# A new order for all 919 steps of an attention and expert-routing kernel

## The chip, the cores and the metric

The kernel runs on one core of a Trainium2 chip. The metric is the device time of one execution in microseconds (us); the median of three runs counts. Engines are named as the profile names them: PE is TensorE (PEld its weight loads), DVE is VectorE, ACT is ScalarE, POOL is GpSimd, SP is SyncE, which issues transfers and computes nothing.

## What is computed

Two stages, all in float32. Attention with sketched features for 4 batches, 4 heads, 1088 tokens and 32 values per head, then a layer of 8 experts in which each of the 4352 tokens goes to one expert:

```python
def phi(x):
    a = np.einsum('rd,bhsd->bhsr', S1, x)          # r = 8
    b = np.einsum('rd,bhsd->bhsr', S2, x)
    return np.einsum('bhsi,bhsj->bhsij', a, b).reshape(*x.shape[:-1], r * r)
q_p, k_p = (phi(q), phi(k))
kv = np.einsum('bhsf,bhsd->bhfd', k_p, v)
z = np.sum(k_p, axis=2)
x = num / den            # num = q_p kv, den = q_p z + 1e-6, as rows of 128
...
logits = x @ w_gate                                 # 128 -> 8
expert_idx = np.argmax(logits, axis=1)
out = gate_w * (np.maximum(x_e @ w1[e], 0.0) @ w2[e])   # 128 -> 1024 -> 128
```

S1 and S2 are float64 and are taken apart into float32 pieces on the chip.

## The kernel before

The kernel is a list of named steps. Each step is a small function that issues a few instructions on fixed engines, and the string `ORDER` at the top of the file names all steps in the order in which they are issued. No scheduler reorders anything: each engine runs its own instructions in the order of that string, and waits where data or a buffer isn't ready. Buffers come from rings (8 PSUM banks, 12 wide buffers of 128 x 1024, 5 buffers for turned rows, and so on), handed out in the order of the string too, so another order also changes which step must be over before a buffer can be used again.

The steps by name:

- `L.…` on SP: a load from HBM. `L.q0`, `L.k1`, `L.v2` are q, k or v of one batch, 512 KB each; `L.kr0a` and the like are the last 64 tokens of a batch, 32 KB; `L.w0` to `L.w7` and `L.x0` to `L.x7` are w1 and w2 of one expert, 512 KB each; `L.fill` writes filler rows into the scratch table. The loads of k of batch 0 (`k0`) stand before the string.
- `S.t`, `S.m`: S1 and S2 are put on the diagonal blocks of a weight (`s_cat`), by two PE transposes (L398) of what a row of DVE instructions made (`s_rep`, L293), and two DVE products (L405).
- `k<batch><half>` and `q<batch><half>` (and `kr`, `qr` for the last tokens): `.t` four PE transposes of the loaded rows (L420), `.x` copy from PSUM (L429 on DVE and L430 on ACT for the first two, ACT alone later), `.a` the products with S1 and S2 on PE (L438), `.l` copy on ACT, `.s` sum on DVE (L453), `.o` outer product on DVE (L466); for k then `.v` on PE (L475, L479), and after a batch's last key the steps `e<batch>`. For q: `.T`/`.U` transposes on PE (L577), `.c`/`.d` copies on ACT, `.n`/`.N` numerators on PE (L595), `.p`, `.e`, `.y` division on ACT and DVE, and `.f`, `.f2` copies of two token columns each into the rows to be routed, on ACT (L622).
- `r<batch>`: routing. `.a` to `.d` give each token its row in a scratch table in HBM that is sorted by expert: `.a`, `.b` on DVE, `.p` on PE (L692, L694), `.d` on DVE (ends with L707), and `.c` (L684 to L686) the gate weight, which stands in the routed row. Then `.s0` to `.s8` scatter the rows, 128 at a time, with indirect transfers on POOL (L713).
- `t<group>` on DVE: which expert and which rows each tile has.
- `j<tile>`: 38 tiles of 128 rows of one expert. Tiles 0 to 9 need the rows of batches 0 and 1, tiles 10 to 17 those of batch 2 as well, later ones all. `.n` reads a row number on SP, `.l` loads and turns the rows (L902), `.g` loads two words of each row (L904), `.c` copies on ACT (L972), `.w` and `.X` copy the expert's w1 and w2 on DVE (L984, L990), `.u` and `.U` are the halves of the first product on PE (L1005), `.r` and `.q` the ReLU on ACT (L1031, L1038) or DVE (L1040), `.d` the second product on PE (L1054), `.y` the scaling on ACT (L1071), `.s` the scatter of the result on POOL (L1076). Tiles 27 to 37 are of two halves of 64 rows each (L1011, L1059).
- `warm` is one PE matmul on zeros after the six of the head; `D0` to `D3` drain POOL; `N2` numbers rows on POOL; `m0.i`, `m1.i` are tiles that run only if they are needed.

The body of a step is short. Two that the prediction speaks of, and the loop that issues them all:

```python
        @op(x + ".l")
        def _():
            if split:
                s["xr"] = xr_bufs.take(2)
                load_rows(j, s["row"], (s["xr"][0:64], slice(0, XW), False))
            else:
                s["t"] = turned_bufs.take()
                load_rows(j, s["row"], (s["t"][:], slice(0, DM), True))
...
    for name in ORDER.split():
        do(name)
```

Of the kernel before, what the change touches and what calls it, by code (L numbers as in the profile page):

```python
# [23 lines left out]
L.k1 k00.o q00.t kr0.a q00.x L.gate q01.x k01.s k11.t L.v0 k01.o kr0.l kr0.s q00.a L.vr0a C.late q00.l L.k3
q01.a L.qr0b q00.s D0 L.v1 k00.v k11.x k01.v kr0.o L.qr0a e0.s q01.l e0.r L.fill e0.k k10.t q00.o k10.x
L.vr1a L.w1 e1.s k11.a q00.U q01.s q01.o q00.T k11.l e0.t C.later e0.c L.qr1a e0.m q01.T q00.c k11.s e0.z
L.q3 q00.d q01.U k10.a q00.N L.q1 q01.c k10.l q01.d q01.n qr0.t L.k2 q00.n q01.p L.q2 q01.N k11.o k10.s
k10.o q00.p2 q01.e q00.e2 L.vr0b qr0.x q00.p q01.y q10.t q11.t qr0.a k20.t q01.p2 q00.y2 q10.x q00.e qr0.l q10.a
q01.e2 q00.y q01.y2 r0.a L.v2 r0.x k10.v k11.v qr0.s q11.x L.kr1b q10.l r0.b q00.f2 k20.x r0.c r0.p L.kr1a
r0.d q10.s e1.r q11.a L.w3 e1.k q11.l k20.a q01.f L.w6 e1.t q00.f q10.o q11.s q10.T qr0.o k20.l q11.o  # L30
q01.f2 q10.U r0.s3 q20.t e1.c e1.m k20.s qr0.T q11.U q20.x qr0.c q11.T L.w0 L.w2 e1.z k20.o q10.c kr1.t
L.v3 qr0.n q10.n L.x2 q11.d qr0.p q11.c L.qr1b q11.N q11.n q10.p q10.d q10.N k21.t qr0.e L.x4 q10.e q11.p2
q10.y q11.e2 q20.a q11.p qr0.y q10.p2 q11.e q11.y2 q20.l q10.e2 r0.s5 L.vr1b r0.s6 r0.s1 kr1.x k21.x r0.s7 q30.t
q11.y q10.y2 r1.a q31.t q11.f2 r1.x kr1.a q21.t k30.t q20.s q11.f kr1.l k21.a L.x1 r1.b q20.o kr1.s k30.x
L.w5 r1.c r0.s4 q10.f2 qr1.t r1.p k30.a r1.d k21.l L.x3 q21.x k20.v k21.s q20.T k30.l qr0.f q20.c kr1.o
e2.s r0.s2 q21.a q30.x k21.o q10.f k21.v q30.a r0.s0 q31.x L.w4 qr1.x k30.s r1.s7 r1.s2 e2.r t0.a k31.t
r1.s1 q20.U q21.l k30.o t0.b e2.k e2.t k31.x k30.v q21.s e2.c k31.a L.w7 q31.a q30.l t0.c q30.s r1.s0
k31.l q21.o e2.m q20.d L.x0 k31.s e3.s e2.z q31.l q30.o q21.U q21.T L.x5 q21.c q31.s q20.n k31.o j8.n
q31.o q20.N q30.T qr1.a q20.p j5.n q21.n qr1.l k31.v q21.p qr1.s e3.r q21.d j5.w q31.U L.x6 e3.k r1.s6
q31.T j7.n q20.e r1.s8 j7.w q30.c e3.t q20.p2 q20.y q21.N r1.s4 j3.n q31.d j9.w e3.m q21.e j0.n q20.e2  # L40
q30.U r1.s3 q21.p2 e3.z q21.e2 j6.n e3.c r1.s5 q30.d j4.n q31.N L.x7 j9.n q30.N qr1.o q21.y q30.p2 q31.c
q30.n q20.y2 j9.l j7.l qr1.T q21.y2 q31.n r2.a j0.l r2.b qr1.c q31.p2 q30.e2 j9.X j9.c qr1.n q31.e2 r2.x
q20.f2 j9.g q30.p r2.p q30.y2 j1.w j3.w j7.c j9.u j9.U D1 j8.w N2 j9.r r2.d j7.u j5.l j0.c
q31.y2 j3.l q20.f j2.n qr1.p j0.X j2.l j0.w qr1.e j4.w q21.f j9.q q30.e j4.X j7.X j7.U j6.l j9.d
q30.f2 j5.c j0.U j3.c r2.c j5.u j7.q j5.g t0.d j5.U j9.y q21.f2 j9.s r2.s6 j7.r t1.a q31.p j1.n
j5.q j5.X j8.l j4.l j1.l j7.g t1.b j5.r t1.c qr1.y q31.e r2.s1 j2.c j0.u j0.q j13.n j3.X j6.w
j6.c q30.y r2.s5 r2.s0 j7.d r2.s7 j0.r j3.U q31.f2 j0.g j6.X j4.c j3.g q31.y j8.c j5.d j2.w j15.n
r3.a j3.u j0.d j6.U j3.q r2.s4 j14.n j1.c j8.u j12.n j0.y j3.r j1.g j1.U q30.f j17.X j10.w j8.U
j6.u j16.n r3.x r2.s3 r3.b j5.y r3.c r3.p j6.g j6.r j16.w j17.w r2.s2 r3.d t1.d j4.u r3.s3 t2.a
j7.y t2.b j10.n j3.d t2.c r3.s1 j4.U qr1.f j2.u q31.f j2.g j8.X j17.n j13.l j6.q j4.r j4.g j2.r  # L50
j17.l j2.U j2.X j17.c j14.w t2.d j10.l j15.w j2.q j4.q j6.d j8.g j17.U j15.l j6.y j2.d j17.u r3.s4
r3.s5 j8.r j18.w r3.s2 j14.l j14.c j17.r j4.d j17.g j20.n r3.s0 j14.u j1.u j22.n j1.X j24.n j17.q j0.s
t3.a j1.q j18.n j11.n t3.b j3.y j14.U j16.l j16.g j17.d j16.c j1.r j16.X r3.s6 r3.s7 j12.l j15.X j10.c
j15.c j26.w j25.n j8.q j26.n r3.s8 j14.r j11.w j18.l j1.d t3.c j17.y j14.X j33.n j33.l j18.c j26.l j1.y
j20.l j15.u j10.u j6.s j15.U j8.d j15.r j26.c j27.n j16.u j16.U j13.X j20.w j14.q j23.n j12.w j18.X j16.q
j22.l j11.l j14.d D2 j16.r j16.d j15.g j29.n j10.g j8.y j31.n j20.c j4.y j20.u j12.X j16.y j20.r j10.U
j10.r j29.l j2.y j19.n t3.d j4.s j15.q j20.X j15.d j20.U j13.w j11.c j31.W j36.n j19.l j18.U j24.g j20.q
j14.g j13.c j31.w j23.l j14.y j26.u j19.c j15.y j11.U j20.g j18.q j20.d j13.U j18.u j31.l j13.g j10.q j22.c
j11.u j26.U j10.X j18.r j32.n j28.n j15.s j11.X j23.c j33.L j11.r j18.d j5.s j29.L j8.s j31.L j33.W j13.q
j27.l j13.u j20.y j34.n j10.d j31.j j1.s m1.w j22.w j12.c j10.y j23.w j12.u j11.q j22.U j2.s j18.g j11.g  # L60
j30.n j21.n j31.o j18.y j26.X j11.d j26.r j29.j j3.s j17.s j29.o j29.X j23.U j27.L j11.y j22.g j32.l j36.l
j12.r j22.u j33.o j37.n j26.q j19.g j13.r j33.j j12.U j13.d j22.q j23.u j26.g j29.W j32.L j34.l j33.b j22.r
j31.b j24.w j24.X j29.b j35.n j21.l j22.X j12.q j31.c j26.d j22.d j21.c j25.X j12.g j33.w j23.q j34.L j19.w
j13.y j12.d j19.X j27.o j36.L j11.s j31.u j31.U j33.c j23.r j20.s j32.o j21.w j33.u j29.w j29.c j31.r j12.y
j22.y j24.l j34.o j33.U j29.U j31.q j26.y j27.w m0.w j29.u j27.j j19.u j32.X j19.U j26.s j32.j j35.l j29.q
j23.X j23.g j24.c j31.X j36.o j16.s j33.X j19.r j31.d j21.u j7.s j33.q j23.d j33.r j24.u j36.j j25.w j35.L
j32.w j30.w j29.r j19.q j28.l j28.L j30.l j24.U j19.d j34.j j25.l j37.l j21.U j21.X j22.s j24.r j28.j j25.c
j35.j j33.d j23.y j24.q j21.r j14.s j25.U j27.W j25.g j37.L j33.y j27.X j31.y j30.L j12.s j25.u j24.d j30.X
# [1104 lines left out]
```

## Time and profile before

| | |
|---|---|
| median of 3 runs | 199.47 us (199.17 to 199.88) |
| the profiled execution's own time | 197.44 us |
| its span, first to last instruction | 195.7 us |
| PE busy | 187.8 us |
| DVE busy | 137.8 us |
| ACT busy | 101.5 us |
| POOL busy | 84.5 us |
| moved by DMA | 23.02 MB |
| granted TensorE clock, mean | 1.00 |

The profiled execution took 1.7 us more than its span and 2.0 us less than the median of the runs. In what follows a time such as "at 62.45" counts from the first instruction of the span. A timeline row gives start, duration, engine, line, operation and names, and in brackets how long the engine stood idle before it and what ended that. Rows that overlap (one engine works on several instructions at a time) are usual: a PE matmul row lasts until its modelled end, while the next one starts well before that.

### The profile page before, as it was taken

To read this page: it belongs to the slowest core of one execution; us is meant where nothing else is said; L and a number is where in the kernel's file an instruction comes from. 1 tells how busy PE (TensorE), PEld (TensorE's weight loads), DVE (VectorE), ACT (ScalarE), POOL (GpSimd) and SP (SyncE) were. 2 spreads that over 40 slices of the span, in tenths; PEclk is the share of its full clock that TensorE was granted. 3 is DMA by queue.
4 is the path that set the end of the run, shared out by engine and by line. 5 is a ranking of instruction groups with operands and counts; after the bars stand their busy time and mean duration, and the time that the engine had idled before them with its cause. 6 is when DMAs were issued, how large, how long until landed. Compare 5 with 4: busy or idle time off the path is not lost.

```text
span 195.7 us, 8926 instructions
## 1 busy us (share of the span) xinstructions
PE 187.8 (96%) x3609; PEld 180.7 (92%) x3609; DVE 137.8 (70%) x406; ACT 101.5 (52%) x255; POOL 84.5 (43%) x106
## 2 busy tenths in 40 slices
PE   7999999998999999999999999999999999999991
...
DMA packets 35660, 23.02 MB, mean 118 GB/s; under 512 B 17155, under 2 KB 33413, under 8 KB 35617
## 3 DMA queue, kind: packets, MB, share of 16 engines
...
q8 instruction: 30, 0.49, 1.1%
...
HBM read 15.84 MB, written 5.05 MB: 107 GB/s over the span
## 4 chain that ended last, share of the span: by engine, by line
PE 69%; DMA 11%; issue 5%; POOL 5%; DVE 3%; ACT 1%; POOLq 1%; SPq 1%; DVEq 0%; ACTq 0%
PE bank L1054 22%; PE bank L1005 21%; PE bank L1011 8%; PE bank L1059 7%; DMA turned<-xs_dram 5%; POOL xs_dram L713 4%; PE bank L438 4%; DMA wide<-in_k_dram 3%; PE bank L420 2%; DMA xs_dram<-x_rows,row_i 2%; PE bank L577 2%; PE bank L475 1%; POOL out_dram L1076 1%; PE bank L595 1%; SPq L902 1%
## 5 line engine op out<-in xcount | busy, mean ns | idle before, releaser
L1076 POOL DMA_INDIRECT out_dram<-y,xg x27 | 29.6, 1096 | 61.2 <-ACT y L1071 55.4
L1005 PE MATMUL bank<-xgT,wide 128*64 128x128 f32 x864 | 51.6, 273 | 0.4 <-ACT xgT L972 0.3
L713 POOL DMA_INDIRECT xs_dram<-x_rows,row_i x34 | 38.6, 1135 | 24.8 <-DVE sum L453 10.4
L1005 PEld LDWEIGHTS bank<-xgT,wide 128*64 128x64 f32 x864 | 47.8, 137 | 0.9 <-ACT xgT L972 0.9
L1040 DVE TENSOR_SCALAR hTb<-bank 128x512 f32<-128x512 f32 x26 | 17.8, 687 | 31.4 <-PE bank L1011 8.5
L984 DVE COPY wide<-w_all 128x1024 f32 x45 | 30.8, 704 | 8.2 <-PE bank L1054 4.4
L1031 ACT ACTIVATE hTa<-bank 128x512 f32<-128x512 f32 x36 | 21.2, 596 | 27.0 <-PE bank L1011 10.4
L1054 PE MATMUL bank<-wide,hTa 128*64 128x128 f32 x432 | 28.3, 273 | 0.2 <-ACT hTa L1031 0.2
L1054 PE MATMUL bank<-wide,hTb 128*64 128x128 f32 x432 | 28.2, 273 | 0.0
L1054 PEld LDWEIGHTS bank<-wide,hTa 128*64 128x64 f32 x432 | 24.3, 137 | 0.7 <-ACT hTa L1031 0.4
L1054 PEld LDWEIGHTS bank<-wide,hTb 128*64 128x64 f32 x432 | 24.5, 137 | 0.0
L990 DVE COPY wide<-w_all 128x1024 f32 x27 | 18.4, 698 | 2.9 <-PE bank L1054 2.2
L466 DVE TENSOR_TENSOR wide<-sum 128x1024 f32<-128x1024 f32 (+1 forms) x18 | 20.2, 1129 | 0.3
L972 ACT COPY xgT<-turned 128x256 uint16<-128x256 uint16 x27 | 12.6, 482 | 13.9 <-DMA turned<-xs_dram 13.8
L438 PE MATMUL bank<-s_cat,xT 128*128 128x128 f32 x136 | 18.5, 280 | 0.2 <-DVE se L684 0.2
L1011 PE MATMUL bank<-xgT,wide 128*64 128x64 f32 x576 | 17.5, 222 | 0.0
L1011 PEld LDWEIGHTS bank<-xgT,wide 128*64 128x64 f32 x576 | 17.3, 138 | 0.2 <-issue 0.2
L438 PEld LDWEIGHTS bank<-s_cat,xT 128*128 128x128 f32 x136 | 16.4, 191 | 0.6 <-ACT x_rows L622 0.2
L1071 ACT ACTIVATE y<-bank,xg 128x128 f32<-128x128 f32 x27 | 9.6, 368 | 11.7 <-PE bank L1054 8.0
L1076 POOL DMA_INDIRECT out_dram<-y,to x11 | 10.8, 978 | 7.7 <-ACT y L1071 5.0
L430 ACT COPY xT<-bank 128x512 f32<-128x512 f32 (+2 forms) x20 | 9.7, 503 | 4.3 <-PE bank L420 4.0
L595 PE MATMUL bank<-kvx,q_pT 128*64 128x82 f32 x272 | 11.5, 237 | 0.1
...
## 6 DMA issues: line engine op xcount, KB each, us to landing
...
xs_dram<-x_rows,row_i POOLq DMA_INDIRECT x34
turned<-xs_dram SPq DMA_TRANSPOSE x27
xg<-xs_dram SPq DMA_DIRECT2D x27, 1.0 KB
```

What stands on the lines that cost most here:

```text
L438: nc.tensor.matmul(t[:, ts(i, 128)], lhsT=st["xT"][:, ts(i, 128)], rhs=s_cat.rearrange("p w t g r -> p (w t g r)"), start=True, stop=True)
L466: nc.vector.tensor_tensor(dst, a[:, :, :, None].broadcast_to([128, n * 4, R, R]), b[:, :, None, :].broadcast_to([128, n * 4, R, R]), ALU.mult)
L713: d = nc.gpsimd.indirect_dma_start(out=xs_dram[:], out_offset=bass.IndirectOffsetOnAxis(ap=st["row"][:, u:u + 1], axis=0), in_=x_rows[b][: ...
L984: nc.vector.tensor_copy(out=s["w1", i], in_=w1_all[:, ds(expert(i), F)])
L990: nc.vector.tensor_copy(out=s["w2"], in_=w2_all[:, ds(expert(0), F)])
L1005: nc.tensor.matmul(t[ts(g, 64), ts(c, 128)], lhsT=s["w1", 0][:, ds((c0 + c) * 128 + g * 64, 64)], rhs=s["xT"], start=True, stop=True, skip ...
L1011: nc.tensor.matmul(t[ts(g, 64), ds(c * 128 + i * 64, 64)], lhsT=s["w1", i][:, ds((c0 + c) * 128 + g * 64, 64)], rhs=s["xT"][:, ts(i, 64)], ...
L1031: nc.scalar.activation(s["hTa"], s["ha"], AF.Relu)
L1040: nc.vector.tensor_scalar(s["hTb"], s["hb"], 0.0, None, ALU.max)
L1054: nc.tensor.matmul(t[ts(i, 64), :DM], lhsT=h[:, ds(c % 4 * 128 + i * 64, 64)], rhs=s["w2"][:, ts(c, DM)], start=(c == 0), stop=(c == 7), s ...
L1059: nc.tensor.matmul(t[ts(i, 64), :DM], lhsT=h[:, ds(c % 4 * 128 + i * 64, 64)], rhs=s["w2"][:, ts(c, DM)] if i else w2_all[:, ds(r + c * DM ...
L1076: d = nc.gpsimd.indirect_dma_start(out=out[:], out_offset=bass.IndirectOffsetOnAxis(ap=s["xg"][:, 1:2].bitcast(I32), axis=0), in_=s["y"], ...
```

## The change

Only the string `ORDER` changes. The same 919 names stand in it, in another order, so that every engine has the same instructions as before in another row. The first line of the string, before and after:

```diff
-warm k00.t k00.x S.t S.m k01.t L.q0 L.kr0a k00.a k01.x L.kr0b k00.l k01.a q01.t k00.s kr0.t k01.l kr0.x
...
+warm S.t k00.t k01.t L.q0 L.kr0b L.kr0a k00.x S.m k01.x L.k1 k00.a L.qr0b k01.a q00.t k00.l L.gate k00.s
```

Three places of it, as the built programs have them.

PE at the head of the program; `wide_73` is k of batch 0, `s_rep` what S1 and S2 became. Before:

```order
L255 MATMUL bank_65<-zeros 128x128 x6
L255 MATMUL bank_66<-zeros 128x128
L420 MATMUL bank_67<-ident,wide_73 128x128 x2
L420 MATMUL bank_68<-ident,wide_73 128x128 x2
L398 MATMUL bank_69<-ident,s_rep_261 128x16
L398 MATMUL bank_69<-ident,s_rep_264 128x16
L420 MATMUL bank_70<-ident,wide_73 128x128 x2
L420 MATMUL bank_71<-ident,wide_73 128x128 x2
L438 MATMUL bank_72<-s_cat,xT_85 128x128 x4
```

and now:

```order
L255 MATMUL bank_65<-zeros 128x128 x6
L255 MATMUL bank_66<-zeros 128x128
L398 MATMUL bank_67<-ident,s_rep_261 128x16
L398 MATMUL bank_67<-ident,s_rep_264 128x16
L420 MATMUL bank_68<-ident,wide_73 128x128 x2
L420 MATMUL bank_69<-ident,wide_73 128x128 x2
L420 MATMUL bank_70<-ident,wide_73 128x128 x2
L420 MATMUL bank_71<-ident,wide_73 128x128 x2
L438 MATMUL bank_72<-s_cat,xT_85 128x128 x4
```

The first four transposes of k (`k00.t`) have moved behind the two of S (`S.t`).

SP's queue of loads from the load of v of batch 0 on (in each line the loaded tensor stands at the right). Before:

```order
L186 DMA wide4_77<-in_v_dram 128x4x256
L191 DMA v_rem_170<-in_v_dram 64x4x32
L186 DMA wide6_79<-in_k_dram 128x4x256
L191 DMA q_rem_169<-in_q_dram 64x4x32
L186 DMA wide7_80<-in_v_dram 128x4x256
L191 DMA q_rem_169<-in_q_dram 64x4x32
L375 DMA xs_dram_166<-x_rows3_182 9x8x1040
L191 DMA v_rem_170<-in_v_dram 64x4x32
L364 DMA w1_all_172<-in_moe_w1_dram 128x1024
L191 DMA q_rem_169<-in_q_dram 64x4x32
L186 DMA wide10_83<-in_q_dram 128x4x256
L186 DMA wide11_84<-in_q_dram 128x4x256
```

and now:

```order
L186 DMA wide4_77<-in_v_dram 128x4x256
L191 DMA v_rem_170<-in_v_dram 64x4x32
L191 DMA q_rem_169<-in_q_dram 64x4x32
L375 DMA xs_dram_166<-x_rows3_182 9x8x1040
L186 DMA wide6_79<-in_q_dram 128x4x256
L364 DMA w1_all_172<-in_moe_w1_dram 128x1024
L191 DMA k_rem_168<-in_k_dram 64x4x32
L186 DMA wide7_80<-in_q_dram 128x4x256
L186 DMA wide8_81<-in_k_dram 128x4x256
L186 DMA wide9_82<-in_q_dram 128x4x256
L186 DMA wide11_84<-in_v_dram 128x4x256
```

Before, k of batch 3, v of batch 1, w1 of expert 1 and q of batch 3 stand ahead of q of batch 1 (`wide11_84`, the last row). Now q of batch 3 (`wide6_79`) and w1 of expert 0 alone stand between v of batch 0 and q of batch 1 (`wide7_80`); k and q of batch 2 follow, then v of batch 1.

POOL from the numbering of batch 2's rows (L239) on; `row_i_2` and `row_i_3` are the scatters of batches 2 and 3, `out_0_dram` those of results. Before:

```order
L239 IOTA x_rows0_223 128x8
L1076 DMA out_0_dram<-y0_154,xg0_107 4352x128
L713 DMA xs_dram_166<-x_rows0_223,row_i_2_1331 39168x130 x8
L713 DMA xs_dram_166<-x_rows3_182,row_i_3_1702 39168x130 x6
L1076 DMA out_0_dram<-y1_155,xg3_110 4352x128
L713 DMA xs_dram_166<-x_rows3_182,row_i_3_1702 39168x130 x3
```

and now:

```order
L239 IOTA x_rows0_223 128x8
L713 DMA xs_dram_166<-x_rows0_223,row_i_2_1327 39168x130 x8
L713 DMA xs_dram_166<-x_rows3_182,row_i_3_1708 39168x130 x4
L1076 DMA out_0_dram<-y0_154,xg2_109 4352x128
L1076 DMA out_0_dram<-y3_157,xg0_107 4352x128
L713 DMA xs_dram_166<-x_rows3_182,row_i_3_1708 39168x130 x5
```

The result of the first tile (`j9.s`) no longer stands ahead of the eight scatters of batch 2.

In the same stretch the other engines read as follows in the string, cut to the steps that matter. PE after the first tile's first product: before `j7.u j7.U j9.d j0.U j5.u j5.U j0.u j7.d j3.U j5.d j3.u j0.d j6.U j8.u j1.U j8.U j6.u r3.p j4.u j3.d j4.U j2.u j2.U j6.d j17.U`, now `j7.U j7.u j9.d j3.U j0.U j3.u j0.u j7.d j8.u j3.d j8.U j6.U j4.U j0.d j4.u r3.p j2.U j6.u j8.d j17.U`. ACT: before `j9.c r2.x q20.f2 q30.p j7.c j9.r j0.c q20.f qr1.p q21.f j9.q q30.f2 j5.c j3.c j7.q j9.y q21.f2`, now `q20.f q31.d q31.p r2.x qr1.c q21.f2 q30.p2 j9.c j7.c qr1.p j9.r j9.q q30.p q21.f q20.f2 j0.c`. DVE: `r2.c` stood 18 steps behind `r2.a`, and now stands 8 behind it. SP's loads of turned rows: before `j9.l j7.l j0.l … j13.l j4.g j17.l`, now `j9.l j7.l j3.l … j14.l j17.l`.

## Rows read from the trace of the kernel before

**Rows 1.** The page: busy tenths of PE in 40 equal slices of the span.

```profile
PE   7999999998999999999999999999999999999991
```

**Rows 2.** Waits of PE's weight loads: who for whom, us in total, times, longest.

```profile
PEld bank L1005 <- ACT xgT L972: 0.9, 2, 0.5
PEld bank L475 <- issue: 0.8, 1, 0.8
...
PEld bank L420 <- DMA wide<-in_q_dram: 0.4, 1, 0.4
PEld bank L1054 <- ACT hTa L1031: 0.4, 1, 0.4
PEld bank L420 <- DMA wide<-in_k_dram: 0.4, 1, 0.4
```

**Rows 3.** Chain that ended last, in order of time: start us, us, what.

```profile
53.19 3.28 DMA xs_dram<-x_rows,row_i
...
57.94 3.96 DMA turned<-xs_dram
61.92 0.49 ACT xgT L972
...
62.45 1.97 PE bank L1005 x32
```

**Rows 4.** Timeline of PE at the head: start, us, engine, line, operation.

```profile
4.21 0.69 PE L420 MATMUL bank<-ident,wide 128*128 128x128 f32 x4
...
5.73 0.66 PE L420 MATMUL bank<-ident,wide 128*128 128x128 f32 x4
6.25 0.49 PE L438 MATMUL bank<-s_cat,xT 128*128 128x128 f32 x2
```

**Rows 5.** Timeline of DVE at the head, and its row at 20.99.

```profile
5.44 0.40 DVE L429 COPY xT<-bank 128x256 f32<-128x256 f32 x1
5.84 0.35 DVE L405 TENSOR_TENSOR s_cat<-bank,mask 128x64 f32<-128x64 f32 x2
...
20.99 0.89 DVE L615 TENSOR_TENSOR heads_of<-bank,den_q 128x320 f32<-128x320 f32 x2 [0.45 <-PE bank L595]
```

**Rows 6.** Timelines: batch 0's last scatter, batch 1's first, DVE's step before it.

```profile
38.09 1.25 POOL L713 DMA_INDIRECT xs_dram<-x_rows,row_i  x1 [0.30 <-issue]
40.69 1.87 POOL L713 DMA_INDIRECT xs_dram<-x_rows,row_i  x1 [1.34 <-issue]
...
39.69 0.23 DVE L707 TENSOR_REDUCE row_i<-rk 128x9 int32<-128x72 f32 x1
```

**Rows 7.** Timeline of POOL: batch 2's first and last scatter.

```profile
68.80 0.98 POOL L713 DMA_INDIRECT xs_dram<-x_rows,row_i  x1 [0.68 <-DVE done L819]
...
78.64 1.01 POOL L713 DMA_INDIRECT xs_dram<-x_rows,row_i  x1 [0.30 <-issue]
```

**Rows 8.** Timelines of DVE (the end of `r2.c`) and ACT (a copy `.f2`).

```profile
67.71 0.21 DVE L686 RECIPROCAL x_rows<-se 128x8 f32<-128x8 f32 x1 [0.23 <-DVE se L685]
...
64.66 0.63 ACT L622 COPY x_rows<-heads_of 128x512 uint16<-128x512 uint16 x1
```

**Rows 9.** Timelines of SP and ACT: tiles 13 and 17 turned, tile 17's copy.

```profile
82.47 1.20 SPq L902 DMA_TRANSPOSE turned<-xs_dram  x1
...
84.50 2.53 SPq L902 DMA_TRANSPOSE turned<-xs_dram  x2
...
87.07 0.49 ACT L972 COPY xgT<-turned 128x256 uint16<-128x256 uint16 x1 [0.48 <-DMA turned<-xs_dram]
```

**Rows 10.** Chain that ended last: one second product, then half a first product.

```profile
69.66 1.75 PE bank L1054 x32
71.40 0.87 PE bank L1005 x16
```

**Rows 11.** Scatters into the table (ns: least, median, most); DVE at 3.05.

```profile
L713 POOL DMA_INDIRECT xs_dram<-x_rows,row_i x34: 966/988/1907, 27.4 to 94.9; - x34
...
3.05 1.44 DVE L272 TENSOR_SCALAR expo_at<-expo 16x32 int32<-16x32 int32 x1
```

More of the change, by code (lines that the diff above doesn't have):

```diff
@@ L22 @@
 ORDER = """
-warm k00.t k00.x S.t S.m k01.t L.q0 L.kr0a k00.a k01.x L.kr0b k00.l k01.a q01.t k00.s kr0.t k01.l kr0.x
[L24 to L68, printed above, removed]
@@ new lines @@
+k01.l kr0.t k00.o L.v0 q01.t k01.s kr0.x L.vr0a kr0.a q00.x kr0.l k01.o q00.a kr0.s q01.x L.qr0a k11.t e0.s
+q00.l q01.a L.fill L.q3 L.w0 k00.v L.kr1b k11.x L.q1 L.k2 k01.v C.late L.q2 D0 kr0.o q00.s e0.r q00.o
+q01.l e0.k qr0.t k11.a L.v1 q01.s e0.t L.vr0b e0.c q01.o k10.t C.later q01.T k11.l k10.x L.k3 L.qr1a L.kr1a
+q01.c q00.U q00.d L.w2 q01.U k10.a k11.s qr0.x e1.s e0.m q01.d L.vr1b e0.z L.w6 L.x1 k11.o q00.T k10.l
+k10.s q01.n q01.N q00.c q01.p k10.o q00.N q01.p2 q00.n q00.p2 q00.p q01.e q01.e2 q10.t qr0.a L.x5 k20.t q11.t
@@ new lines @@
+q10.x qr0.l q01.y q01.y2 q00.e2 q00.e L.qr1b q01.f q00.y2 q00.y L.v2 q20.t q11.x r0.a r0.x q10.a qr0.s k20.x
+r0.b r0.c k10.v r0.p q11.a r0.d r0.s4 q01.f2 L.x3 k11.v q10.l e1.r L.w7 q10.s k21.t q11.l q00.f e1.k
+k20.a e1.t r0.s0 q10.o qr0.o q11.s q20.x k20.l q11.o e1.c r0.s6 qr0.T e1.m q00.f2 q10.T q11.U k20.s q11.T
+q10.U qr0.c q10.c L.x4 e1.z q11.d qr0.n qr0.p q11.N q10.n q11.c q11.p2 q10.d k20.o q11.n q10.p q11.p q10.N
+L.v3 r0.s1 qr0.e qr0.y q11.e2 q11.y2 L.w1 qr1.t q10.e kr1.t q10.y q20.a k21.x q10.p2 L.w3 q11.e q20.l q11.y
@@ new lines @@
+q10.e2 q30.t k30.t q21.t L.vr1a qr0.f q10.y2 r1.a kr1.x q20.s k30.x r1.b q10.f k21.a r1.x k31.t q20.o r1.p
+k31.x q11.f r0.s2 L.w4 L.x7 kr1.a r1.d r0.s7 k21.l q10.f2 k31.a r0.s3 r1.c q20.T r0.s5 k21.s t0.a q31.t
+k20.v q20.c r1.s5 L.w5 q30.x kr1.l q21.x kr1.s k30.a e2.s q21.a k21.o k30.l k21.v q11.f2 k30.s q30.a L.x6
+e3.s L.x2 q21.l q31.x t0.b r1.s1 kr1.o q21.s qr1.x t0.c e2.r q20.U j6.n q30.l k30.o q30.s e2.k r1.s3
+e2.t q21.o k31.l j8.n q31.a k30.v k31.s e2.c q21.T e2.m q21.U q20.d e2.z q30.o r1.s7 q20.N k31.o q31.l
@@ new lines @@
+q21.d qr1.a q31.s j9.w j3.n q20.n q21.N q30.U q21.c k31.v q21.p2 j3.w j4.n j9.n qr1.l j5.n j2.n r1.s0
+e3.r r1.s6 q30.T r1.s2 q21.e2 j1.n L.x0 q31.o e3.k q20.p2 r1.s8 j0.n q20.e2 q20.p qr1.s e3.t qr1.o q30.d
+q21.n q21.y2 e3.m q31.T q20.e j7.n q21.p e3.z q20.y2 q31.U e3.c q20.y q30.N q21.e q30.c q21.y q31.c r1.s4
+r2.a j9.l q20.f q31.n qr1.T q30.n q31.d q31.p q31.e D1 r2.b q31.N r2.x j7.l r2.p q31.y j3.l qr1.c
+q21.f2 q30.p2 j0.l j9.c qr1.n j7.w j9.X j7.c j9.u j9.U qr1.p j6.l j9.r j0.g j9.q r2.d q30.p j7.U
@@ new lines @@
+j7.u j9.d j3.g q21.f q30.e2 r2.c qr1.e j0.w N2 q20.f2 j8.l q30.y2 t0.d j0.c t1.a j7.X j4.l j7.q
+j3.c j8.w t1.b q30.e j3.U j0.U j3.q t1.c j3.u r2.s2 j7.r j2.l q30.y r2.s1 j8.c j17.n r2.s5 q31.p2
+j0.q qr1.y r2.s4 j3.X r2.s6 j3.r j5.l j12.n q31.e2 j4.c j0.X j0.u q30.f2 j9.g qr1.f j15.n j5.g j13.n
+j7.g j6.g r2.s0 j7.d j8.u j1.g q31.y2 j6.w j15.w j3.d j2.w j8.r j14.n j8.U j6.c j2.X j4.w r2.s3
+j5.c j6.U j8.X j0.r j6.q j1.l j2.c j4.U j5.w j0.d r3.a q31.f2 j9.y j1.c j4.q r2.s7 r3.b j14.l
+j17.l j11.w j11.X j17.w j4.u j8.q q30.f j16.n j6.X r3.p j2.U r3.x j7.y j17.c j6.u t1.d r3.d j8.d
@@ new lines @@
+j13.w j17.U j4.X j12.l j6.r t2.a j13.l j15.l j17.g q31.f j6.d j17.q r3.c j1.w r3.s4 j17.X j4.g j13.c
+j2.u j4.r t2.b j17.u j10.n j2.q j15.c j4.d r3.s2 t2.d j8.g r3.s5 j6.y j1.U j17.r t2.c t3.a j15.u
+j12.g r3.s3 j17.d j12.c j0.y j2.r t3.b t3.c j9.s j11.n j0.s j16.l j5.u r3.s8 r3.s7 j5.X r3.s1 j10.l
+j26.w j11.l j16.c j3.y j13.u j5.U j18.n j18.w j17.y r3.s0 j16.w j2.g j13.U j11.c j13.r r3.s6 j4.y j14.g
+j24.n j5.r j33.n j11.U j1.q j20.n j21.n j6.s j5.q j1.u j19.n j23.n j13.X j18.l j15.U j2.d j5.d j15.r
@@ new lines @@
+j25.n j10.c j19.l j23.l j31.n D2 j26.n j1.X j10.w j16.X j11.g j18.g j28.n j31.l j2.y j29.W j1.r j14.w
+j15.q j29.n j11.u j18.c j12.w j16.U j16.u j1.d j13.q j29.w j14.X j8.y j13.g j22.n m0.w j15.g j16.r j16.q
+j13.d j5.y j18.X j23.w j11.r j29.l j11.q j10.U j23.c j16.d j10.u j15.X j12.u j14.c j26.l j30.n j15.d j18.U
+t3.d j1.y j11.d j10.q j12.r j11.y j31.L j10.X j10.g j13.y j10.r j14.U j20.l j12.U j14.u j26.c j22.l j33.l
+j36.n j18.u j33.L j26.U j20.w j22.w j14.q j10.d j32.n j27.n j24.l j15.y j22.c j31.j j26.q j26.u j26.X j8.s
```

19 lines of the change are left out of this document (14 added, 5 removed).

## The prediction, made before the changed kernel ran

> **What bounds the kernel now.** I read the page's slices first. PE is at nine tenths or more in all but three of the 40 slices [rows 1], so the time is its start, its work, the little that it waits and a tail, and an order that changes no instruction can win only waits. Next the waits of its weight loads, which stand at the head of each group of matmuls and so show when PE lacked something. The five largest waits behind the head are 0.9, 0.8, 0.4, 0.4 and 0.4 us, 2.9 us together [rows 2]: about 1.5% of the time, and the most that this change can gain outside head and tail.
>
> Then the chain that ended last, to see who sets those waits. In the attention half it runs through POOL: the scatters of batches 0 and 1, one train of 17, then their landing, the turned load of an expert tile, ACT's copy and PE at 62.45, the second tile's first product [rows 3]. From there PE works almost without a gap to the end, so a microsecond at 62.45 is a microsecond at the end, unless a later wait eats it. The last thing to read is when the next group of tiles, 10 to 17, can be loaded, since these need batch 2's scatters. The tail (last product, scaling, five scatters, landing) holds the same steps in both orders; I take 0 for it.
>
> The sum is made against the profiled execution, 197.44 us. The median of the runs is 199.47, 2.03 more, and I add that at the end. A measurement of this kernel can tell 0.3%, 0.6 us, from no change.
>
> **Head: PE starts 0.72 us later.** Now PE does four transposes of k at 4.21, while DVE still prepares S, and the other four from 5.73, and its first real product starts at 6.25 [rows 4]. With S first, the first four move to 5.73 and the others behind them. By the length of those rows (0.66 us for four) I estimate that the first pair is out at about 6.11. DVE's copy of that half (0.40) and the products that make `s_cat` (0.35) come in this order [rows 5], so `s_cat` is ready at about 6.91, and the product starts at 6.97 instead of 6.25.
>
> **Loads: 0.8 us of waits go.** PE waited 0.4 us for q of batch 1 and 0.4 us for k of batch 2 [rows 2]. Counting 512 KB loads from the start, q of batch 1 was the ninth and is the seventh, k of batch 2 was the tenth and is the eighth. Both waits should close, even with nothing else gained. q of batch 2 is now the ninth and v of batch 1 the tenth, where the ninth and tenth now land just when PE stands at `q10.t` and `k20.t`; PE comes to `q20.t` four and to `k10.v`, the first use of v of batch 1, six steps after `q10.t`, so neither is late. Head and loads together: -0.1 us at the point where the waits were. If the head's loss stayed in full, DVE's steps would carry it on to the scatters below.
>
> **Batch 1's scatters: 0.3 us earlier.** Batch 0's last scatter ended at 39.34 and batch 1's first began at 40.69, after 1.34 us of idling; ordinary idling is 0.30 [rows 6]. It waited for DVE, whose last step ended at 39.92, 0.77 us before. DVE comes there 0.72 later by the head, 0.45 earlier by the wait at 20.99 [rows 5] that goes with the loads, and some 0.2 earlier since one small sum now stands behind it; at best 0.7 more of small gaps close. So the scatters start between 40.04 and 40.76: 0.65 earlier to 0.07 later. I take 0.35 earlier, near the middle, and put PE's 62.45 at 62.1. The instruction fetch that held PE for 0.8 us at line 475 [rows 2] lies beside this train and is taken at zero either way; without that cover it costs or saves up to 0.8.
>
> **Batch 2's scatters: 3.7 us earlier, and needed 5 us earlier.** Before, the train of eight started at 68.80, behind the first tile's result on POOL and behind `r2.c`, which ended at 67.92 [rows 7, 8]. Now nothing of tile 9 stands ahead of it, and `r2.c` is ten steps earlier on DVE, some 4 us. The last thing the first scatter waits for is `q20.f2` on ACT. ACT starts tile 7's copy at 61.92 now [rows 3] and is through the copy, two ReLUs, two row copies and two short ones by 64.66 [rows 8]; the new order has the same kinds in that stretch with one copy fewer. Less the 0.35, that is 64.3. With 0.77 to the first scatter [rows 6] it begins at 65.1.
>
> Today's train has its last start 9.84 us after its first, 1.41 each; at its shortest a scatter takes 0.98 and 0.30 of idling, 1.28 [rows 7]. So the last starts at 74.1 to 74.9. The first turned load of the group followed 3.83 us after the last start (78.64 to 82.47), a second load follows after 1.35, and tile 17's copy started 2.57 after its load [rows 9]; PE starts 0.53 after such a copy (61.92 to 62.45) [rows 3]. That makes tile 17's `.U` possible at 82.4 to 83.2.
>
> PE now comes to it sooner. Between the second tile's start and `j17.U` it did 26 us of work; in the new order 13 halves of 0.87, 5 second products of 1.75 [rows 10] and the routing product, some 0.6: 20.7 us. From 62.1 that is 82.8. So data and PE meet within half a microsecond; I take 82.9. The old kernel had the same amount of work behind it at 62.45 + 20.7 = 83.15. **So the change is 0.25 us ahead there.**
>
> **After that 0.8 us more.** The second of the two waits for turned rows (0.9 in total less the 0.5 at 62.45) and the wait for a ReLU that was stuck behind such a copy, 0.4 each [rows 2], belonged to tiles 14 and 16, whose loads came 3 us after tile 17's and were needed at once. In the new order tiles 15, 13, 11 and 16 follow at 7 to 20 us behind `j17.U`, with loads 1.35 apart; by the same steps each has 1.4 us or more to spare. Batch 3's rows are needed some 30 us later, and `r3.c` may slip by 3 us unseen. DVE's copies of weights are in time by their order in the worst case I found (`j4.w`, about a microsecond ahead). All other moves I take at zero, with their ends at the largest single wait of today, 0.9, either way: every step has a new neighbour, and a new wait of that size needs no special reason.
>
> **The sum:** -0.25 - 0.8 = -1.05; 197.44 - 1.05 = 196.4 in the profile, and with 2.03 **198.4 us**. By the ends of the terms this case alone spans 197.8 to 199.1.
>
> **Rivals.**
>
> *Batch 2's scatters come too late: slower.* The new order has 5.3 us less work to cover their train. If the train is no earlier than now, tile 17 is ready at 82.47 + 1.35 + 2.57 + 0.53 = 86.9, 3.75 us late; less the 0.8 that is 202.4. If it starts on time but each takes as long as in batch 1's train, (53.19 - 40.69) / 8 = 1.56 [rows 3, 6], `j17.U` comes at 84.2: 199.7. The point from which it decides is 1.52 us a scatter. For it: the train now runs beside weight copies on DVE, scatters took up to 1.91 us, and at 3.05, while POOL filled buffers, a DVE step on 16x32 values lasted 1.44 us [rows 11], so the two engines can hold each other up. Against it: today's train also ran beside a busy DVE, at 1.41. I put it at 201.
>
> [...]
>
> *No change.* Batch 1's train starts no earlier (its upper end), tile 17 is half a microsecond late, and the fetch or one of the new neighbours takes back the rest: 199.4. That the order doesn't do what it was searched for belongs here: where the fetches fall among the loads can't be read from it.
>
> *More.* Every term at its good end, the wait of 0.5 at 62.45 gone as well: -0.65 - 0.8 - 0.5, 197.5.
>
> **Chances.** The forecast 0.45, too late 0.20, no change 0.27, more 0.08. Of the forecast's 0.45, 0.38 lies below 198.87 and counts as faster, with "more" and a little of "no change" 0.48. Within 0.3%: 0.07 of the forecast, 0.22 of "no change", 0.02 of the late train, 0.31. Slower 0.21. The range 197.2 to 201.0 leaves out the worst half of the late train and the last of "more".
>
> **What would show it.** The first L438 at about 6.97. No wait of L420 for q or k. Batch 1's first scatter near 40.3. Batch 2's first scatter near 65.1 and its last near 74.5. PE's `j17.U` near 82.9, with no wait of L1005 for a copy above 0.5 and none of L1054 for a ReLU. Wrong would be a train of batch 2 that begins later than 66 or needs over 11 us, or a new wait of a microsecond in the middle of the tiles.

## The result and the profile after

The changed kernel is slower: median 201.66 us over 20 runs (199.81 to 203.11) against 199.38 us over 20 runs of the kernel before on the same chip, a ratio of 1.0121 with an interval of 1.0094 to 1.0148. Forecast was 198.4 us, with a range of 197.2 to 201.0.

| | before | after |
|---|---|---|
| median | 199.38 us | 201.66 us |
| profiled execution, own time | 197.44 us | 201.70 us |
| its span | 195.7 us | 199.9 us |
| PE busy | 187.8 us | 190.1 us |
| POOL busy | 84.5 us | 83.0 us |
| first L438, start | 6.25 | 7.55 |
| batch 1's first and last scatter, start | 40.69, 53.19 | 43.24, 55.25 |
| second tile's first product | 62.45 | 64.55 |
| batch 2's first and last scatter, start | 68.80, 78.64 | 67.38, 77.27 |
| last scatter of a result, start | 192.00 | 196.21 |

The two profiled executions differ by 4.3 us, the medians by 2.3: the profile of before lies 1.9 under its median, that of after on it. So the profiles tell where time went, and the ratios how much. Two of the five sets of runs below met chips whose granted clock was 0.86 to 0.93 in every execution, those of the kernel before too (267 to 275 us): of these runs only the head is read, and their ratios (0.976 to 0.984 for five runs of a_tail, a_all and a_best, 1.011 and 1.019 for b_warm2 and b_warm2b) are not used.

The slices of the changed kernel's page, to be laid beside [rows 1]:

```profile
PE   6999999999999999999899999999999999999990
...
DVE  5399998899998899888899585557484365160210
...
POOL 8010018768820475007771103861001017787453
```

PE is as full as before. POOL is busy at seven to eight tenths from 170 to 185, which will matter for the tail.

**The head.** Timeline of PE in the changed kernel, against [rows 4]:

```profile
1.06 3.35 PE L255 MATMUL bank<-zeros 128*128 128x128 f32 x14 [1.06 <-DVE zeros L201]
5.25 0.61 PE L398 MATMUL bank<-ident,s_rep 16*128 16x16 f32 x2 [0.83 <-DVE rest L298]
5.79 1.97 PE L420 MATMUL bank<-ident,wide 128*128 128x128 f32 x8
7.55 2.88 PE L438 MATMUL bank<-s_cat,xT 128*128 128x128 f32 x16
10.27 0.60 PE L420 MATMUL bank<-ident,wide 128*128 128x128 f32 x4
```

The order of the rows is the forecast's, their lengths are not. Eight transposes take 1.97 us, where four took 0.66; their starts lie 0.213 us apart, the next group's (at 10.27) 0.109. The trace's first record of the granted clock, at full speed, stands at 9.49; in the kernel before at 4.38. In both the pace changes there: the starts of L438 lie 0.213 apart up to 9.47 and 0.111 to 0.112 from 9.60 on, and in the kernel before the transposes from 4.41 on lie 0.109 to 0.110 apart, behind warm-up matmuls at 0.213. So PE did this work at about half the pace of the kernel before. What PE did ahead of it: the warm-up ends at 4.4, and it stood idle for 0.83 us until S came. Before, it went from the warm-up into k's transposes without a pause.

**Batch 1's scatters.** Timeline of DVE in the changed kernel where batch 1's routing ends, against [rows 6]:

```profile
41.65 0.23 DVE L707 TENSOR_REDUCE row_i<-rk 128x9 int32<-128x72 f32 x1
...
42.25 0.22 DVE L686 RECIPROCAL x_rows<-se 128x9 f32<-128x9 f32 x1
```

and of POOL, batch 0's last scatter and batch 1's first:

```profile
40.00 1.98 POOL L713 DMA_INDIRECT xs_dram<-x_rows,row_i  x1 [0.30 <-issue]
43.24 0.97 POOL L713 DMA_INDIRECT xs_dram<-x_rows,row_i  x1 [1.26 <-ACT q_pT L583]
```

The gate weights (`r1.c`, ending with L686) now stand behind the row numbers (`r1.d`, ending with L707), and the scatter needs both. It starts 0.77 after the end of L686 at 42.47, as it started 0.77 after L707 in the kernel before. The bracket names ACT's copy L583, which ended at 43.12. In a_best4 below that copy ended at 42.50, when the first scatter had long started (40.27, again 0.77 after DVE's last step), so the scatter doesn't wait for it.

**The middle.** Waits of PE's weight loads in the changed kernel (who for whom, us in total, times, longest), against [rows 2]:

```profile
PEld bank L1005 <- ACT hTa L1031: 1.4, 1, 1.4
...
PEld bank L1005 <- ACT xgT L972: 0.6, 1, 0.6
```

The chain that ended last, from 78 to 101 us (start us, us, what):

```profile
78.67 2.38 DMA turned<-xs_dram
...
81.68 3.54 DMA turned<-xs_dram
85.22 0.02 issue
85.24 0.48 ACT xgT L972
85.72 0.04 issue
85.77 1.09 PE bank L1005 x16
...
94.83 4.42 DMA turned<-xs_dram
99.25 0.02 issue
99.27 0.02 ACT xgT L972
99.29 0.32 issue
99.62 0.59 ACT hTa L1031
100.21 0.04 issue
100.25 0.76 PE bank L1005 x9
```

No wait for q or k is left, as forecast. The wait of 0.6 is tile 17 at 85.77. The wait of 1.4 is new: tile 11's turned rows, asked for at 94.83, came 4.42 us later; ACT stood at their copy, behind it stood tile 13's ReLU, and PE had no free bank for tile 11's product until that ReLU was done.

**The tail.** ACT's last scaling in the kernel before, in the timeline of ACT:

```profile
191.34 0.37 ACT L1071 ACTIVATE y<-bank,to 128x128 f32<-128x128 f32 x1 [2.22 <-PE bank L1059]
```

and POOL's scatters of results there, the last ones ahead of the drain and behind it:

```profile
181.75 0.97 POOL L1076 DMA_INDIRECT out_dram<-y,to  x1 [0.30 <-issue]
186.62 0.97 POOL L1076 DMA_INDIRECT out_dram<-y,to  x1 [3.90 <-ACT y L1071]
...
192.00 0.97 POOL L1076 DMA_INDIRECT out_dram<-y,to  x1 [0.30 <-ACT y L1071]
```

The same of ACT in the changed kernel:

```profile
194.73 0.37 ACT L1071 ACTIVATE y<-bank,to 128x128 f32<-128x128 f32 x1 [2.22 <-PE bank L1059]
```

and of POOL in the changed kernel, where the scatters from 165.29 to 186.74 stand 0.30 apart:

```profile
165.29 0.97 POOL L1076 DMA_INDIRECT out_dram<-y,xg  x1 [1.81 <-ACT y L1071]
166.57 1.05 POOL L1076 DMA_INDIRECT out_dram<-y,xg  x1 [0.30 <-issue]
...
186.74 0.97 POOL L1076 DMA_INDIRECT out_dram<-y,to  x1 [0.30 <-issue]
191.10 0.97 POOL L1076 DMA_INDIRECT out_dram<-y,to  x1 [3.38 <-issue]
...
196.21 0.97 POOL L1076 DMA_INDIRECT out_dram<-y,to  x1 [0.30 <-issue]
```

Before, the last scatter starts 0.29 after the last scaling's end (191.71). Now it starts 1.11 after it (195.10). The wait of 3.38 ahead of 191.10 is the drain `D3`: its record (L1102) lasts from 184.10 to 190.24, 3.50 past the start of the last scatter ahead of it, at 186.74. In the kernel before it lasts from 180.71 to 185.77, 4.02 past 181.75. The last five results then stand in one train of 1.28 us each.

### The profile page after: what moved, and what is told of

Read it like the earlier page. It is cut to its first block, busy times and chain, and to the rows that moved or that the text cites. A ratio compares the mean times of both kernels' runs of the same rounds, so it can differ in the third digit from the quotient of the medians.

```text
span 199.9 us, 8946 instructions
## 1 busy us (share of the span) xinstructions
PE 190.1 (95%) x3609; PEld 182.2 (91%) x3609; DVE 138.8 (69%) x406; ACT 101.1 (51%) x255; POOL 83.0 (42%) x106
## 4 chain that ended last, share of the span: by engine, by line
PE 49%; DMA 15%; issue 10%; POOL 7%; SPq 5%; DVE 5%; ACT 4%; POOLq 2%; ACTq 0%; DVEq 0%
PE bank L1054 19%; PE bank L1005 16%; DMA turned<-xs_dram 11%; POOL out_dram L1076 5%; PE bank L1011 3%; PE bank L1059 3%; POOL xs_dram L713 3%; DMA k_rem<-in_k_dram 2%; PE bank L438 2%; DVE wide L466 2%; SPq L191 2%; DMA xs_dram<-x_rows,row_i 2%; PE bank L595 1%; PE bank L420 1%; PE bank L577 1%
## 5 line engine op out<-in xcount | busy, mean ns | idle before, releaser
L713 POOL DMA_INDIRECT xs_dram<-x_rows,row_i x34 | 39.2, 1152 | 44.6 <-ACT lo L448 14.2
L1076 POOL DMA_INDIRECT out_dram<-y,xg x27 | 27.2, 1007 | 50.6 <-ACT y L1071 44.2
L984 DVE COPY wide<-w_all 128x1024 f32 x45 | 31.4, 712 | 9.5 <-PE bank L1011 5.5
L438 PE MATMUL bank<-s_cat,xT 128*128 128x128 f32 x136 | 19.9, 291 | 0.1
L990 DVE COPY wide<-w_all 128x1024 f32 x27 | 18.9, 710 | 1.4 <-PE bank L1054 1.3
L438 PEld LDWEIGHTS bank<-s_cat,xT 128*128 128x128 f32 x136 | 17.7, 202 | 0.8 <-ACT xT L430 0.6
```

The costliest lines, as they stand in the source:

```text
L438: nc.tensor.matmul(t[:, ts(i, 128)], lhsT=st["xT"][:, ts(i, 128)], rhs=s_cat.rearrange("p w t g r -> p (w t g r)"), start=True, stop=True)
L713: d = nc.gpsimd.indirect_dma_start(out=xs_dram[:], out_offset=bass.IndirectOffsetOnAxis(ap=st["row"][:, u:u + 1], axis=0), in_=x_rows[b][: ...
L984: nc.vector.tensor_copy(out=s["w1", i], in_=w1_all[:, ds(expert(i), F)])
L990: nc.vector.tensor_copy(out=s["w2"], in_=w2_all[:, ds(expert(0), F)])
L1076: d = nc.gpsimd.indirect_dma_start(out=out[:], out_offset=bass.IndirectOffsetOnAxis(ap=s["xg"][:, 1:2].bitcast(I32), axis=0), in_=s["y"], ...
```

## The experiments

The theory after this reading: three separate losses, at the head (about 2.1 us in the profile), in the middle (the wrong order of turned loads) and in the tail (0.8). The rival: the train of scatters sets the pace, and what is repaired at one place the next wait takes. `a_…` starts from the changed order, `b_…` from the kernel before.

**The head put back, PE kept busy, the head alone.**

```diff
 a_oldhead
-warm S.t k00.t k01.t L.q0 L.kr0b L.kr0a k00.x S.m
+warm k00.t k00.x S.t k01.t L.q0 L.kr0b L.kr0a S.m
 a_warm10
-WARM = 6
+WARM = 10
 b_newhead
-warm k00.t k00.x S.t S.m k01.t
+warm S.t k00.t k01.t k00.x S.m
```

> The changed order with one thing put back: the first four transposes of k and their copies stand ahead of S again, as in the kernel before. Theory (head): PE goes from the warm-up straight into k at 4.21, its matmuls run about 0.11 us apart from there, the first L438 starts at 6.25 instead of 7.55, and the 2.1 us of the head come back whole, since nothing later in the changed order has slack to swallow them: batch 1's first scatter near 41.2, the second tile's first product near 62.5, median 199.6, 0.1% over the kernel before. Rival (rest of the order): the head's loss is swallowed by later waits, and the waits in the middle and the tail set the time: 201 or more.

Measured: 1.0053 (1.0018 to 1.0088) of the kernel before; first L438 at 6.25, batch 1's first scatter at 41.42, second tile at 63.03. The head is back to the hundredth, and 0.7% of the 1.2% with it, give or take 0.4. 0.5% stays, which lies between the two: the head is part of the loss, and something behind it is the rest.

> The kernel before with one thing of the change: both transposes of S stand ahead of all of k's, all else as before. Theory (head): first L438 near 7.55, matmuls 0.21 us apart until about 9.3, and 2.1 us more at the second tile's first product (64.5) and at the end: 201.5, 1.0% over. Rival (only the 0.7 us that the order costs by itself): 200.1, 0.35% over. Rival (the old order has slack that swallows it): 199.4.

Measured: 1.0071 (1.0036 to 1.0105). The rise came at 4.48 this time, and PE's timeline in b_newhead reads:

```profile
5.73 1.09 PE L420 MATMUL bank<-ident,wide 128*128 128x128 f32 x8
6.95 2.05 PE L438 MATMUL bank<-s_cat,xT 128*128 128x128 f32 x16
...
62.25 1.97 PE L1005 MATMUL bank<-xgT,wide 128*64 128x128 f32 x32 [0.24 <-ACT xgT L972]
```

Same steps, same pause of 0.82, and at full clock (eight transposes in 1.09 us, in the changed kernel 1.97): 6.95, where the forecast had 6.97. So 0.7 us is what the order costs at the first L438, and in the changed kernel's profile a late clock came on top, 0.6 up to there. At the second tile nothing of it is left in this profile: 62.25, where the kernel before had 62.45 and the theory 64.5. This execution is also the fastest of the twelve (198.14 us, their median 199.70). So the time shows that the new head costs something, and the profile doesn't show how that reaches the end.

> The changed order as it is, but ten warm-up matmuls on zeros instead of six, so that PE is busy from 1.06 until S is ready near 5.25. It computes the same. Theory (clock): PE's clock goes up near 4.4 as in the kernel before, because PE hasn't stood idle ahead of it; the eight transposes and sixteen L438 from 5.8 on are 0.11 us apart and not 0.21, the first L438 starts near 7.0, the second group of L420 near 8.9 instead of 10.27; 1.4 us come back, 0.7 stay lost to the order alone: median 200.3. Rival (order alone): PE waits for S either way, more warm-up changes nothing: 201.7, with the transposes 0.21 apart as before.

Measured: rise at 4.17, first L438 at 6.95, next L420 at 8.84: the head as expected. The time not: 1.011 (1.0053 to 1.0167), six runs of 199.0 to 201.6 us, where 0.45% was expected. That is a miss: without the late clock the time is that of the changed kernel, as far as six runs can tell. It would fit if most executions of the changed kernel had an early clock anyway, so that the mean gain is a fraction of 1.4, but no run shows that.

> The changed kernel once more, unaltered, to see whether its head repeats. In its first profile PE's full clock was granted at 9.49, in the two other orders with S first at 4.48 and 4.92. Theory (chance): the clock's rise after PE's pause is not the same in every execution, so it may now be near 4.5 to 5, with the first L438 at 6.95, or again near 9.5 with 7.55. Rival (fixed): it is 9.5 again, within 0.3, and what differed in the two other orders was something else. The time against the kernel before: 1.2% over by either.

Measured (head only): rise at 9.00, L438 at 7.56, eight transposes again in 1.97 us. Over all seven executions with S first and the pause, the first rise stood at 9.49, 9.00, 4.92, 4.48, 4.42, 4.99 and 3.96 (in the last it fell again at 7.37). It was late in two of seven, both of them the changed kernel unaltered; the rival's second rise, 9.5 within 0.3, fails by 0.2. The three executions of a_tail, early at 4.42, 3.96 and 4.99, differ from the changed kernel only far behind the head, which speaks for chance. It isn't shown, since both executions of the changed kernel itself were late.

**A pause made on purpose** in the kernel before: `WARM = 2` instead of 6. Run three times (of b_warm2 and b_warm2b only the head is read).

> The kernel before with two warm-up matmuls instead of six at its start and nothing else changed; it computes the same. PE then stands idle from about 2.5 until k is there near 4.2. Theory (a pause of PE ahead of its work makes its clock rise late): full clock is granted only well after 4.4, the first transposes and L438 start 0.21 us apart, and the kernel loses 1 to 2 us at the head, 0.5 to 1.0% over. Rival (the clock rises a fixed time after the start, whatever PE did): rise near 4.4, L438 0.11 apart from 6.25 on, no change.

> The kernel of b_warm2 again, for a chip at full clock. Theory (a pause ahead of PE's work makes the clock rise late, and the loss is carried to the end): rise near 9 to 10, first L475 near 13.5, 1.5 us or 0.75% over the kernel before. Rival (the old order swallows a late head): 0.3% over or less.

Measured: rise at 10.2, 8.53 and 11.14. PE's timeline in b_warm2c:

```profile
1.06 1.65 PE L255 MATMUL bank<-zeros 128*128 128x128 f32 x6 [1.06 <-DVE zeros L201]
3.69 1.09 PE L420 MATMUL bank<-ident,wide 128*128 128x128 f32 x4 [0.98 <-POOL v_rem L232]
...
6.69 3.62 PE L438 MATMUL bank<-s_cat,xT 128*128 128x128 f32 x16
```

After a short warm-up and a pause the clock rose late in all three, and the rival of a fixed time falls. Which of the two did it, the shorter warm-up or the pause, these runs don't separate. The time of b_warm2c: 1.0043 (1.0009 to 1.0076), 0.9 us, a little over half of what the theory said. In its profile the first L475 stood at 14.42, 2.5 later than before, the second tile at 65.12, 2.7 later, and the span was 2.2 us longer, but the profile of before lies under its median. How much of a late head is carried to the end stays open.

**The middle.** Two loads of turned rows ahead of others on SP; for a_best also two steps on ACT.

```diff
 a_turned, a_all, a_best
-… j14.l j17.l … j16.l … j10.l j26.w j11.l
+… j17.l j14.l … j11.l j16.l … j10.l j26.w
 a_best
-… j16.c … j11.c j13.r
+… j13.r j11.c j16.c
```

> The changed order with two loads of turned rows moved ahead on SP: tile 17's ahead of tile 14's, and tile 11's ahead of those of tiles 16 and 10. Theory (tile loads in the wrong order): the wait of 0.67 us for tile 17's copy at 85 and the wait of 1.43 us at 98.8 behind tile 11's copy both go, PE reaches 105 about 2 us earlier and nothing else is late at once: 199.7, 0.15% over the kernel before. Rival (batch 2's scatters set the pace): tile 17 still waits, since its load can't start before the last scatter has landed, and the tiles that were moved back now wait instead: 201 to 201.7.

Measured: the waits for tile 17 and behind tile 11, 0.64 and 1.41 by the rows of the weight loads, shrank to 0.32 and 0.54 in the profile, but the time is 1.0127 (1.007 to 1.0185), no gain. A miss for the theory by its number, though six runs can't tell 0.5%.

**The tail.** Five scatters moved ahead on POOL, into a stretch of idling.

```diff
 a_tail, a_all, a_best
-… j20.s … j18.s … j10.s … j16.s … j3.s … j12.s
+… j18.s j10.s j16.s j3.s j12.s j20.s
```

The runs that count are a_tail3, a_all3 and a_best3, the third of the first two kernels and the second of the last:

> The changed order with five scatters of results (of tiles 18, 10, 16, 3 and 12) moved ahead of that of tile 20 on POOL, where POOL stood idle for 16.5 us before. Theory (backlog on POOL): in the changed kernel POOL scatters without a pause from 165 to 188, so the drain after it ends at 190, the last five scatters begin at 191.1 and the last one starts 1.1 us after the last scaling on ACT; with five fewer in that train the drain ends earlier than the last tile's scaling, the last scatter starts 0.3 after the last scaling as in the kernel before, and 0.8 us go: 200.9, 0.8% over the kernel before. Rival (the last five scatters and their landing take what they take): no change, 1.2% over, and the last scatter still 1 us behind the last scaling.

> The kernel of a_tail a third time (the changed order, five scatters of results moved ahead on POOL), for a chip at full clock. Theory (backlog on POOL): last scatter about 0.3 after the last scaling instead of 1.1, 0.8 us less than the changed kernel, 0.8% over the kernel before. Rival: no change, 1.2% over, last scatter 1 us behind the last scaling.

Measured: 1.0077 (1.0035 to 1.0118), 0.44% less than the changed kernel; by the two intervals that difference is uncertain by 0.5%, so the time alone doesn't show a gain. The timeline of POOL in a_tail3 reads as the theory said:

```profile
182.52 0.97 POOL L1076 DMA_INDIRECT out_dram<-y,to  x1 [0.30 <-issue]
187.33 0.97 POOL L1076 DMA_INDIRECT out_dram<-y,to  x1 [3.84 <-ACT y L1071]
...
192.76 0.97 POOL L1076 DMA_INDIRECT out_dram<-y,to  x1 [0.30 <-ACT y L1071]
```

The drain now ends before ACT has scaled the first result behind it (the wait of 3.84 ends with ACT), and the last scatter starts 0.28 after the last scaling's end (192.11 + 0.37). In the same profile the wait behind tile 11 isn't there at all, with the middle as the changed order has it: its rows came in 2.7 us (92.43 to 95.11).

> The kernel of a_all a third time (old head, turned loads of tiles 17 and 11 ahead, five scatters ahead), for a chip at full clock. Theory (three separate losses): from 1.2% over, less 0.7% for the head, 0.4% for the tail and 0.5% for the turned loads: 0.4% under the kernel before. Rival (the tiles wait for the scatters of batches 2 and 3 whatever stands at the head): 0.3% over or more.

> The kernel of a_best again (a_all, and on ACT tile 13's ReLU and tile 11's copy ahead of tile 16's copy), for a chip at full clock. Theory (ACT's order holds what is left of the waits): no wait of PE above 0.4 between 80 and 105, 0.6% under the kernel before. Rival (the turned loads land late by themselves): the same as a_all3 within 0.2%.

Measured: a_all3 1.0018 (0.9985 to 1.0051), a_best3 1.0006 (0.997 to 1.0043). PE's longest wait between 80 and 105 is 0.44 in the one and 0.25 in the other. With head, tail and middle put right the new order is level with the kernel before: the 1.2% is accounted for to within some 0.4, but the 0.4 to 0.6% under the kernel before is not there, and the step on ACT is worth nothing that can be measured.

**What became of the loads.** The kernel before with q of batch 1 and k of batch 3 exchanged on SP, and k of batch 2 and w1 of expert 1.

```diff
 b_loads
-… L.k3 … L.w1 … L.q1 … L.k2
+… L.q1 … L.k2 … L.k3 … L.w1
```

> The kernel before with two pairs of loads exchanged on SP: q of batch 1 now stands where k of batch 3 stood and the reverse, k of batch 2 where w1 of expert 1 stood and the reverse; all else as before. It has the earlier loads of the changed order without the rest of it. Theory (DVE sets the pace between 14 and 36): the two waits of PE for q and k, 0.4 each, are gone from the rows, but waits for DVE take their place, batch 1's first scatter stays within 0.3 of 40.7 and the time within 0.2% of the kernel before. Rival (the term of the forecast): 0.8 us less lost by PE at 30, batch 1's first scatter near 40, 0.4% under.

Measured: 0.9976 (0.9947 to 1.0004), between the two. Both waits for q and k are gone, and PE reaches its first tile at 59.81 instead of 60.21. But the second tile comes at 62.69 instead of 62.45, after a wait of 1.15 instead of 0.51. The chain that ended last in b_loads (start us, us, what):

```profile
54.09 2.67 DMA xs_dram<-x_rows,row_i
...
58.23 3.91 DMA turned<-xs_dram
62.14 0.02 issue
62.16 0.49 ACT xgT L972
62.65 0.04 issue
62.69 1.31 PE bank L1005 x20
```

Batch 1's first scatter started at 40.47, 0.22 earlier, and the last at 54.09, 0.90 later. In this profile PE spends what the loads give it on waiting for the scattered rows; DVE as the taker, my theory, isn't shown. Nor is it shown that the exchange made the train longer: it takes 13.6 us from first to last start here, 12.5 in the profile of before, and 13.2 in those of b_newhead and b_warm2c, which leave this stretch of the order alone. The interval of the time has room for all of the 0.8 us and for none.

**The train started earlier.** As a_best, with `r1.c` ahead of `r1.d` and `q20.o` (1.22 us on DVE) behind both, `q20.T` two steps later.

> As a_best, and in the routing of batch 1 the gate weights stand ahead of the row numbers on DVE, and q of batch 2's outer product of 1.22 us behind both (its transposes on PE two steps later). Theory (batch 1's scatters wait for DVE's last step, 0.77 us behind it in every run, and that step now ends 0.9 earlier): first scatter of batch 1 near 40.5 where a_best had 41.38, the second tile's first product near 62.0 instead of 62.90, the wait of 0.56 ahead of it gone, 0.3 to 0.4% under the kernel before. Rival (PE waits instead for that outer product, or the scatter is held by POOL's own train, whose batch 0 ends at 40.2): the same as a_best within 0.2%.

Measured: 1.0047 (1.0018 to 1.0076), no gain; that it is 0.4% over a_best3 the two intervals don't settle. The first scatter came at 40.27, as expected. The last started at 53.41, against 53.39 in a_best3, and the second tile's product at 63.82, against 62.90. PE came late by itself: it waited 0.9 us at 41.6 and 0.6 at 49.5 for what follows the moved outer product, and at the second tile it no longer waited for rows. The first of the two in PE's timeline of a_best4:

```profile
42.55 0.38 PE L438 MATMUL bank<-s_cat,xT 128*128 128x128 f32 x1 [0.68 <-ACT q_pT L583]
```

The first rival holds, and in this profile the train that started 1.1 earlier ended no earlier. I found no version that is shown to beat the kernel before.

## Why the prediction was wrong

It named the right places and had the price of several steps right. But three things that it put at nothing weren't nothing (matmuls 0.213 us apart at the head where 0.109 was counted on, the spare of the turned loads, the tail), and the gain of the loads was counted at a point where b_loads doesn't show it. Both of its signs of being wrong came: batch 2's train began later than 66, at 67.38, and there is a new wait of over a microsecond, behind tile 11. The rival that put a late train at 201 came near the measured 201.66 by luck: its train was late by itself or slow, while here it was as long as forecast and late with everything ahead of it.

In the profile the miss is 5.3 us (201.70 for 196.4). Of these, 2.9 stand at `j17.U` (85.77 for 82.9), and 2.45 of them already at the second tile (64.55 for 62.1); the wait behind tile 11 is 1.4 and the tail 0.8. By its steps:

- **Head.** "The product starts at 6.97 instead of 6.25": the order's share was right, 6.94 to 6.96 in every execution with an early clock. The step that failed is that all rows were priced at the pace of [rows 4], four transposes in 0.66 us. In both profiles of the changed kernel PE stood idle for 0.83 and 0.85 us between warm-up and work and then started its matmuls 0.213 us apart until about 9, which took 1.2 to 1.4 us more (the next L420 at 10.04 and 10.27, with an early clock at 8.84). That the pause makes the clock late isn't shown: with it the rise was late in two of seven executions, without it and with six or more warm-up matmuls in none of ten (6.29 at the latest). By the times the head costs 0.7% (a_oldhead, b_newhead), uncertain by 0.3 to 0.4. How that divides between order and clock is open: with an early clock the new head reached the second tile at 62.95 (a_turned), no later than the old head in a_oldhead (63.03).
- **Loads.** "Both waits should close": they did. "Head and loads together -0.1" failed: by the times the head alone cost 0.7%, some 1.4 us. Of the loads' 0.8, b_loads shows 0.4 at the first tile and nothing at the second in its profile, and 0.24% in its time, which may be nothing.
- **Batch 1's scatters 0.3 earlier.** They began 2.55 later, and 0.73 later with the old head. The step that failed took L707 as the last that the scatter waits for; in the new order that is L686, 0.59 later, and DVE comes to the routing late besides (its first step, L659, started at 37.76 instead of 35.15). The price of 0.77 from DVE's end to the scatter held in both kernels. In a_best4 an earlier start didn't bring an earlier end.
- **Batch 2's scatters.** Their place was right: the first was forecast 3.0 behind the second tile's start (65.1 and 62.1) and came 2.83 behind it (67.38 and 64.55), 0.78 after ACT's copies ended at 66.60, with the train at 9.89, where 9.84 was today's. The rival that feared 1.52 a scatter didn't come. The eight took 0.97 to 1.36 us each, none of them near its 1.91, beside eleven copies of weights on DVE (L984, L990). The loads behind them failed: I took 2.57 us from a turned load to its copy, the single row of tile 17 in [rows 9]. Here it was 3.56 for tile 17 and 4.44, 4.69, 3.20 and 2.68 for tile 11 in four executions (the changed kernel, a_oldhead, a_warm10, a_tail3).
- **"After that 0.8 us more."** The waits of tiles 14 and 16 went. "Each has 1.4 us or more to spare" failed by the same row: 2.57 and 1.4 make 3.97, and in the two executions with over 4.4 PE waited 1.41 and 1.69, in the two others nothing.
- **The tail at 0.** "The same steps in both orders" is true of the steps behind the last product, not of what stands ahead of the drain on POOL: 0.82 us in the profile, 0.44% in the time of a_tail3, which is uncertain by 0.5%.

Two points of its working change nothing of this. The five waits of [rows 2] aren't the five largest, since L962 and L531 wait 0.5 us each in the same view, so the bound of 2.9 was a microsecond too low. And the 0.8 us at line 475 ends with "issue" in the same view: two transfers of the instruction queues stand between 44 and 47 us, and that they held PE there is the prediction's estimate. In the changed kernel's rows that wait is 0.2.

By the runs: 1.2% in all, of which 0.7% came back with the old head and 0.4% with the tail, the latter not clear of the noise, and a middle whose mean share is too small to be told. With all three put right the new order is level with the kernel before, so the 1 us of gains didn't arrive. Which later wait took it no run shows.
